# A cached attention block on one core: K loaded by pairs of packs in 16 KB rows, the query weights loaded without a staging copy

## The chip, the cores and the metric

The kernel runs on one core of a Trainium2 chip. The metric is device time in microseconds of one execution. Besides the times there is a profile of one execution: a trace of every instruction, of the DMA packets and of the semaphores.

## What is computed

Two independent blocks A and B, each an attention layer with a cache, their outputs side by side:

```
B, Sq, D = 16, 64, 640;  H, Sk, Dh = 32, 512, 128        # all bf16
q = (x @ wq).reshape(B, Sq, H, Dh).transpose(0, 2, 1, 3)
scores = einsum("bhqd,bhkd->bhqk", q, k_cache) * Dh ** -0.5
p = softmax(scores, axis=-1)
o = einsum("bhqk,bhkd->bhqd", p, v_cache)
out_block = o.transpose(0, 2, 1, 3).reshape(B, Sq, H * Dh) @ wo
out = concatenate([out_A, out_B], axis=-1)
```

K and V are 67 MB each per block, 268 MB in all; every byte of them is used once. wq and wo are 5.2 MB each per block.

## The kernel before

**Tiling.** The work is cut into 128 packs. A pack is 4 heads of 2 batches: 8 pairs of head and batch, 1 MB (1,048,576 bytes) of K and as much of V. Four packs (NJ = 4) make a group, which shares one tile of x (2 batches, 128 rows of queries). Eight groups, 32 packs, make a phase: all 16 batches for 16 of the 32 heads of a block. There are four phases (A, A, B, B), and each has its own half of wq and wo: 2.6 MB of each.

**The steps of a pack n**, by the kinds under which the planner lists them:

- QP (L688, TensorE): q from xT and wq, 20 matmuls; QE (L694, ScalarE) copies it out.
- KT (L702, VectorE): K of the pack, 128 x 2048 words of 4 bytes, is transposed in blocks of 32 x 32 from kn_ring to kt_ring. A word is two neighbouring bf16 of one key.
- S (L712, TensorE): the scores; EX (L741, ScalarE): exp with row sums; RC (VectorE): reciprocals; NM (L762, POOL): normalization.
- TR (L774, TensorE): transposes of the normalized pack; TE (L854, VectorE, two copies): pT from PSUM.
- PV (L867, TensorE): times V; OE (L875) and ZO (L879, ScalarE).
- OP (L887, TensorE): times wo, summed up over the four packs of a group; OS (L897, L900, VectorE) takes the sum once per group.

**Order of work.** Nothing is scheduled at run time. `build_plan` gives each step a time in units of packs (the table AT: KT of pack n at n - 0.672, S at n, TR at n + 1.293, TE at n + 1.432 and n + 1.47, PV at n + 1.701, and so on), sorts each engine's list by it, and works out the semaphore waits from what each step reads and writes. Each engine works through its list in order. TensorE's and ScalarE's lists run as loops of four packs.

**Loads.** All loads but the first x are issued by SP, in order of a list of their own (`loads`). V of pack n stands at n - 2.1 and waits for the ring of four V buffers: for PV of pack n-4, told by the end of the TR of pack n-3. K of pack n stands at n - 4.6; its ring kn_ring has six packs. From pack 8 on, a pack's K is two DMAs of 512 KB in rows of 8 KB, and V is one DMA of 1 MB in rows of 4 KB; packs before 8 have four and two smaller ones. wo is loaded per pack and phase (L621, 640 KB).

**wq** is loaded in five DMAs per phase, in rows of 4 KB, to a staging tile ws_sb (L615). The step WP (L656, POOL, 1.26 us) copies it, twice for each of the four packs of a group, to wqp_sb with its columns in another order; QP reads wqp_sb. The five loads of a later phase are spread over the phase before; those of the first phase are the first loads of all.

**The layout.** In a pack, partition 4 (h p) + 2 b + l of kn_ring holds 32 keys of one head and batch: a row of 8 KB. The columns of wqp_sb are ordered so that q's rows match the order in which the transpose leaves the columns of K.

**Zeroing.** Before the first pack VectorE zeroes two V buffers (VZ, L594), four PSUM banks (BZ, L598), half of wo_sb (WZ, L602) and pT (TE of pack -2, L852), so that steps for the packs -2 and -1, which don't exist, do no harm. POOL zeroes one pn buffer (NM of pack -1, L760).

After the last pack of the main program the kernel looks at a flag and would run a second, more general program if row sums were out of range; here it isn't run.

Of the kernel before, what the change touches and what calls it, by code (L numbers as in the profile page):

```python
# [20 lines left out]
class Cfg:  # L21
    NK = 6
    NV = 4
    NKT = 2
# [9 lines left out]
    NARROW = 2  # L34
    AFTER = 24
# [5 lines left out]
              OPZ=(1.65, 1.7), OSH=(1.75, 1.8), STH=(1.85, 1.9), FL1=1.3, FLM=1.68, FLC=1.82, WP0=(-1.6, -1.59, -0.7, -0.69, 0.25, 0.26, 1.25, 1.26),  # L41
              WP1=(-3.5, -2.55, -2.45, -1.5, -0.5, 0.5, 0.6, 1.5))
# [44 lines left out]
def build_plan(dims, cfg, general):  # L87
# [7 lines left out]
    AT = cfg.AT  # L95
    ops = []
# [9 lines left out]
    def add_output(n):  # L106
# [27 lines left out]
        for b in range(2):  # L134
            add("dve", "TE", (n, b), n + AT["TE"][b], [], [("B", 4 + b), ("pT", b, 0), ("pT", b, 1)])
# [36 lines left out]
    for ph in range(NPH):  # L172
        twp = [ph * PH + t for t in AT["WP1" if ph else "WP0"]]
        for kt in range(dims["KT"]):
            ready = (twp[-1] - PH if ph > 1 else AT["WP0"][-1]) + 0.5
            op = add("sp", "LDWQ", (ph, kt), twp[0] - 0.5 if ph else -20.0, [], [("ws", kt, j) for j in range(NJ)])
            loads.append((ready + 2.0 + 0.14 * PH * kt if ph > 1 else AT["PV"] + 0.15 if ph else -50.0, 1, op))
        for j in range(NJ):
            w = ph * NJ + j
            n0 = ph * PH + j  # L180
            for i in range(2):
                add("pool", "WP", (w, i), twp[2 * j + i], [("ws", kt, j) for kt in range(dims["KT"])], [("wqp", j, i)])
            if ph:
                loads.append((n0 - NJ + AT["LDWO"], 4, add("sp", "LDWO", w, n0 + AT["OP"] - 0.8 * NJ, [], [("wo", j)])))
            else:
                loads.append((n0 - 1.9, 4, add("sp", "LDWO", w, n0 + AT["OP"] - 0.8 * NJ, [], [("wo", j)])))
    if not general:
        add("pool", "PZ", 0, -9.95, [], [("zeros",)])
    add("dve", "VZ", 0, -9.9, [], [("v", i % cfg.NV, b) for i in (-2, -1) for b in range(2)])
    add("dve", "BZ", 0, -9.8, [], [("B", 4), ("B", 5), ("B", 6), ("B", 7)])  # L190
    add("dve", "WZ", 0, -9.7, [], [("wo", NJ - 2), ("wo", NJ - 1)])
    add("pool", "NM", -1, -1 + AT["NM"][3], [], [("pn", -1 % cfg.NPN, i) for i in range(4)])
    for n in range(-2, N):
# [4 lines left out]
        add("pe", "QP", n, n + AT["QP"], [("xT", g % cfg.NX), ("wqp", j, 0), ("wqp", j, 1)], [("SB", 1)])  # L198
        add("act", "QE", n, n + AT["QE"], [], [("SB", 1), ("qs", n % cfg.NQ)])
        for i in range(4):  # L200
            if i < 2 or n < cfg.KSPLIT:
                op = add("sp", "LDK", (n, i), n + AT["KT"] - 0.9, [], [("kn", n % cfg.NK)])
                loads.append((n - cfg.NV + AT["PV"] + 0.2 - cfg.KLEAD, 2, op))
        add("dve", "KT", n, n + AT["KT"], [("kn", n % cfg.NK)], [("kt", n % cfg.NKT)])
        add("pe", "S", n, n + AT["S"], [("qs", n % cfg.NQ), ("kt", n % cfg.NKT)],
# [47 lines left out]
    for op in ops:  # L253
# [9 lines left out]
        if op.kind == "QP" and op.idx > 0:  # L263
            op.deps = [d for d in op.deps if d.kind != "WP"]
# [3 lines left out]
    def for_pe(d):  # L268
        if d.kind == "EX":
            return d.idx % 4 == 1 or d.idx % 4 == 0 and d.idx // 4 % NJ == 1  # L270
        if d.kind == "OE":
            return d.idx[1] == 0
        if d.kind == "LDV":
            return d.idx[1] == 1
        if d.kind == "NM":
            return d.idx % 4 == 3 and d.eng == "pool"
        if d.kind == "OS" and d.idx == N // NJ - 1:
            return False
        return d.kind in own

    def stand_in(d, op):
        if op.eng == "pe":
# [4 lines left out]
            if d.kind == "OE":  # L287
                return d if d.idx[1] == 0 else at[("ZO", d.idx[0])]
            if d.kind in ("EX", "MX") and not for_pe(d):
                if op.kind == "S":  # L290
                    return at[("QE", op.idx)]
                return d if id(op) not in inside and d.kind == "EX" else None
            return d
        if d.kind == "PV" and op.eng == "sp":
            return at[("TR", d.idx + 1)]
        if d.kind == "QP" and op.eng == "pool":
            return at[("TR", d.idx - 1)]
        if d.kind == "XT" and op.eng == "sp":
            return at[("XE", d.idx)]
        if d.kind == "OS" and op.eng == "sp" and for_pe(d):  # L300
            return at[("RC", (d.idx * NJ + NJ + 1, 1))]
        if not for_pe(d):
# [3 lines left out]
        if d.kind == "KT":  # L306
            return at[("S", d.idx)]
# [34 lines left out]
    for op in ops:  # L342
        if op.kind == "LDK":
            packs.setdefault(op.idx[0], []).append(op)
            op.group = packs[op.idx[0]]
# [159 lines left out]
def mha_kernel(nc, blocks, out, cfg=None):  # L505
# [18 lines left out]

    plans = []
# [6 lines left out]
    with contextlib.ExitStack() as es:  # L532
# [5 lines left out]
        wqp_sb = sb("wqp_sb", [128, NJ, KT, 512], BF16)  # L538
        wo_sb = sb("wo_sb", [128, HPH, D], BF16)
        ws_sb = sb("ws_sb", [128, KT, NJ, 512], BF16)  # L540
        kn_ring = sb("kn_ring", [128, NK, 2, 2048], BF16)
        kt_ring = sb("kt_ring", [128, NKT, 32, 2, 2, 16, 2], BF16)
# [68 lines left out]
        def em_LDWQ(e, op):  # L611
# [3 lines left out]
            ins = e.dma_start(ws_sb[:, i].rearrange("p j c -> p (j c)"), src[:, i, c:c + NJ * 512])  # L615
# [8 lines left out]
        def em_LDK(e, op):  # L624
            n, b, l = op.idx[0], op.idx[1] // 2, op.idx[1] % 2
            blk, bp, j, h = pack_info(n)
            src = blocks[blk][1][2 * bp:2 * bp + 2, h:h + 4].rearrange("b h (p l t) d -> l (h p) b (t d)", l=2, t=32)[l]
            if n < cfg.KSPLIT:
                ins = e.dma_start(kn_ring[2 * b + l::4, n % NK].rearrange("p a c -> p (a c)"), src[:, b])
            else:  # L630
                ins = e.dma_start(kn_ring[l::2, n % NK].rearrange("p a c -> p (a c)"), src)  # L631
            return ins, ins

        def em_LDV(e, op):
# [15 lines left out]
            return ins, ins  # L650

        def em_WP(e, op):
            j, jj = op.idx[0] % NJ, op.idx[1]
            src = ws_sb[:, :, j].rearrange("p k (i j r) -> p k i j r", i=4, j=2)
            dst = wqp_sb[:, j].rearrange("p k (i r j two) -> p k i j r two", i=4, j=2, two=2)
            ins = e.tensor_copy(dst[:, :, :, jj], src[:, :, :, jj].rearrange("p k i (r two) -> p k i r two", two=2))  # L656
# [23 lines left out]
        def em_QP(e, op):  # L680
# [4 lines left out]
            w = wqp_sb[:, j].rearrange("p k (c f) -> p k f c", f=4)  # L685
# [12 lines left out]
        def em_KT(e, op):  # L698
            n = op.idx
            dst = kt_ring[:, n % NKT].rearrange("p t j b k two -> p (t j) b (k two)").bitcast(F32)  # L700
            src = kn_ring[:, n % NK].rearrange("p a c -> p (a c)").bitcast(F32).rearrange("p (c h b l) -> p c h b l", h=8, b=2, l=2)
            ins = e.transpose(dst.rearrange("p c b (h l) -> p c h b l", h=8, l=2), src)  # L702
            return ins, ins

        def em_S(e, op):
            n = op.idx
            first = last = None
            for f in range(4):
                for b in range(2):
                    for i in range(4):  # L710
                        rows = slice(32 * i, 32 * i + 32)
                        last = e.matmul(ps[64 * b:64 * b + 64, i, :], qs_ring[rows, n % NQ, f, b, :],  # L712
                                        kt_ring[rows, n % NKT, :, f // 2, b, :, f % 2],
# [16 lines left out]
        def exp_views(h):  # L730
            u = 2 if wide(h // 4) else 4
            return (ps[:, h % 4, :].rearrange("q (u t p) -> q t p u", u=u, p=16),
# [199 lines left out]
        ahead = {}  # L932

# [3 lines left out]
        def emit(e, op, p, taken):  # L937
# [3 lines left out]
            if waits and not op.dma and op.kind != "FL1":  # L941
                attach = waits.pop()
            for s, v in waits:
                e.wait_ge(sem[s], v * units(s))
            kind = "EXG" if p and op.kind == "EX" else op.kind
            first, last = emitters[kind](e, op)
            if last is None:
# [123 lines left out]
```

## Time and profile before

| | |
|---|---|
| median of 3 runs | 732.01 us (731.84 to 732.11) |
| the profiled execution | 732.12 us |
| its span, first to last instruction | 730.4 us |
| mean granted TensorE clock | 0.99 |
| TensorE busy | 674.1 us (92%) |
| VectorE busy | 514.5 us (70%) |
| ScalarE busy | 533.3 us (73%) |
| POOL busy | 417.9 us (57%) |
| moved by DMA | 295.02 MB, mean 404 GB/s |

The span is cut into 40 slices on the page; a digit is the busy share of a slice in tenths. L702 and the like are line numbers of the kernel before. In a row of the order of time stand start, length, engine, line, operation, out<-in, shape and count, and in brackets how long the engine was idle before it and what ended that. The chain of waits follows the work that ended last back to what released it. The profile's DMA share is the mean busy share of the 16 DMA engines that move all data.

### The profile page before, as it was taken

What the parts mean: (1) busy time and instruction counts of PE and PEld (TensorE: products, weight loads), DVE (VectorE), ACT (ScalarE), POOL (GpSimd) and SP (SyncE); (2) the same over time, 40 slices, a digit from 0 to 9 for tenths busy, and PEclk for the clock granted to TensorE, in tenths of its full rate; (3) what the DMA queues carried; (4) which work ended last, traced back from release to release, by engine and by line L of the source; (5) the groups of instructions that cost most, each with busy time, mean ns of one, the idle gap of its engine ahead of it and who ended that gap; (6) DMA issues with size and microseconds to landing.
All of it is one profiled execution on the core that took longest, in us unless ns stands there. A gap on an engine that the chain in (4) does not pass through costs nothing.

```text
span 730.4 us, 61195 instructions
## 1 busy us (share of the span) xinstructions
PE 674.1 (92%) x28502; PEld 530.3 (73%) x28502; DVE 514.5 (70%) x691; ACT 533.3 (73%) x1574; POOL 417.9 (57%) x596
## 2 busy tenths in 40 slices
PE   1679999999999999999997899999999799999998
PEld 1458778787777777777775677787777577787775
DVE  5447777777777766767765667677777567878775
ACT  1447878778787777777875677777778677878775
POOL 4436565666875455554884555465587446555552
PEclk9889999999999999999999999999999999999999
DMA  8999999999999999999999999999999999999993
GB/s 337 401 404 414 414 415 413 415 414 415 415 400 409 419 414 416 416 416 417 416 411 402 415 414 413 414 415 415 414 416 407 403 415 418 417 418 417 416 415 122
DMA packets 72336, 295.02 MB, mean 404 GB/s; under 512 B 7664, under 2 KB 20080, under 8 KB 55920
## 3 DMA queue, kind: packets, MB, share of 16 engines
q1 hardware_dynamic: 72160, 294.52, 100.0%
q8 instruction: 10, 0.16, 0.1%
q10 hardware_dynamic: 144, 0.16, 0.1%
q14 instruction: 22, 0.18, 0.1%
HBM read 292.03 MB, written 2.62 MB: 403 GB/s over the span
## 4 chain that ended last, share of the span: by engine, by line
PE 53%; DMA 32%; SPq 6%; DVE 3%; issue 3%; POOL 2%; ACT 1%; DVEq 0%; POOLq 0%
DMA xn_ring<-in_B_x_dram 14%; PE ps L867 12%; PE ps L887 11%; PE ps L688 11%; PE ps L712 10%; DMA kn_ring<-in_A_k_cache_dram 9%; PE ps L774 7%; DMA kn_ring<-in_B_k_cache_dram 5%; DMA wo_sb<-in_B_wo_dram 4%; SPq L631 4%; DVE kt_ring L702 2%; POOL pn_ring L762 2%; SPq L641 1%; DVE pT_sb L854 1%; SPq L615 1%
## 5 line engine op out<-in xcount | busy, mean ns | idle before, releaser
L762 POOL TENSOR_SCALAR pn_ring<-pn_ring,recip 128x512 bf16<-128x512 bf16 x508 | 343.4, 695 | 246.1 <-DVE recip L754 221.0
L702 DVE STREAM_TRANSPOSE kt_ring<-kn_ring 128x2048 f32<-128x2048 f32 x128 | 295.3, 2307 | 120.3 <-DMA kn_ring<-in_B_k_cache_dram 80.3
L741 ACT ACTIVATE pn_ring<-ps 128x512 bf16<-128x512 f32 x512 | 296.4, 592 | 5.7 <-PE ps L712 5.7
L854 DVE COPY pT_sb<-ps 128x1024 bf16<-128x1024 bf16 x256 | 168.4, 671 | 60.2 <-PE ps L774 60.2
L688 PE MATMUL ps<-xT_ring,wqp_sb 128*128 128x128 bf16 x2560 | 165.9, 220 | 11.6 <-POOL xT_ring L677 11.6
L867 PE MATMUL ps<-pT_sb,v_ring 32*128 32x64 bf16 x16448 | 162.2, 192 | 10.6 <-DVE pT_sb L854 4.6
L688 PEld LDWEIGHTS ps<-xT_ring,wqp_sb 128*128 128x128 bf16 x2560 | 157.5, 114 | 17.8 <-issue 11.8
L867 PEld LDWEIGHTS ps<-pT_sb,v_ring 32*128 32x128 bf16 x16448 | 147.0, 91 | 24.8 <-issue 12.5
L887 PE MATMUL ps<-wo_sb,oT_sb 128*128 128x320 bf16 x1024 | 163.5, 303 | 0.0
L875 ACT ACTIVATE oT_sb<-ps 128x256 bf16<-128x256 f32 x257 | 84.7, 381 | 95.1 <-PE ps L867 95.1
L712 PE MATMUL ps<-kt_ring,qs_ring 32*64 32x512 bf16 x4096 | 138.4, 380 | 4.8 <-issue 4.8
L694 ACT ACTIVATE qs_ring<-ps 128x512 bf16<-128x512 f32 x128 | 76.4, 597 | 76.5 <-PE ps L688 74.5
L774 PEld LDWEIGHTS ps<-ident,pn_ring 64*128 64x128 bf16 x4096 | 68.3, 95 | 77.0 <-ACT oT_sb L875 46.0
L887 PEld LDWEIGHTS ps<-wo_sb,oT_sb 128*128 128x128 bf16 x1024 | 90.4, 98 | 36.7
L741 ACT ACTIVATION_READ_ACCUMULATOR pn_ring<-ps 128x1 f32 x512 | 105.3, 206 | 0.0
L774 PE MATMUL ps<-ident,pn_ring 64*128 64x64 bf16 x4096 | 82.9, 191 | 22.8 <-POOL pn_ring L762 18.6
L712 PEld LDWEIGHTS ps<-kt_ring,qs_ring 32*64 32x64 bf16 x4096 | 53.4, 103 | 32.9 <-issue 5.5
L754 DVE RECIPROCAL recip<-rowsum 128x2 f32<-128x2 f32 x256 | 40.6, 158 | 27.6 <-ACT pn_ring L741 24.6
L879 ACT ACTIVATE ps<-zeros 128x256 f32<-128x256 bf16 x128 | 49.5, 387 | 4.1
L656 POOL COPY wqp_sb<-ws_sb 128x1280 bf16<-128x1280 bf16 x32 | 39.6, 1256 | 9.9 <-DMA ws_sb<-in_A_wq_dram 6.8
L668 ACT ACTIVATE xe_sb<-ps 128x640 bf16<-128x640 bf16 x32 | 22.9, 716 | 8.7 <-PE ps L662 8.6
L677 POOL COPY xT_ring<-xe_sb 128x640 bf16<-128x640 bf16 x16 | 11.5, 717 | 21.0 <-PE ps L774 21.0
(42 smaller groups left out, 103.5 us busy)
## 6 DMA issues: line engine op xcount, KB each, us to landing
kn_ring<-in_B_k_cache_dram SPq DMA_DIRECT2D x128, 512.0 KB, 16.1
v_ring<-in_B_v_cache_dram SPq DMA_DIRECT2D x62, 1024.0 KB, 16.5
kn_ring<-in_A_k_cache_dram SPq DMA_DIRECT2D x112, 512.0 KB, 11.4
v_ring<-in_A_v_cache_dram SPq DMA_DIRECT2D x56, 1024.0 KB, 14.8
kn_ring<-in_A_k_cache_dram SPq DMA_DIRECT2D x32, 256.0 KB, 8.6
v_ring<-in_A_v_cache_dram SPq DMA_DIRECT2D x16, 512.0 KB, 8.9
ws_sb<-in_A_wq_dram SPq DMA_DIRECT2D x10, 512.0 KB, 9.3
wo_sb<-in_A_wo_dram SPq DMA_DIRECT2D x8, 640.0 KB, 13.3
```

The costliest lines, as they stand in the source:

```text
L688: last = e.matmul(ps[:, 1, f * 128:(f + 1) * 128], w[:, kt, f, :], xT_ring[:, xs, kt, :], start=(kt == 0), stop=(kt == KT - 1))
L694: ins = e.activation(qs_ring[:, op.idx % NQ].rearrange("p f b q -> p (f b q)"), ps[:, 1, :], ACTF.Copy, scale=scale)
L702: ins = e.transpose(dst.rearrange("p c b (h l) -> p c h b l", h=8, l=2), src)
L712: last = e.matmul(ps[64 * b:64 * b + 64, i, :], qs_ring[rows, n % NQ, f, b, :], kt_ring[rows, n % NKT, :, f // 2, b, :, f % 2], start=(f = ...
L741: ins = e.activation(dst, src, ACTF.Exp, scale=1.0, accum_out=sum_of(h))
L762: ins = e.tensor_scalar(pn_view(h), pn_view(h), recip[:, h:h + 1], 1.0, ALU.mult, ALU.mult)
L774: last = e.transpose(pt_bank(b)[:, 64 * c:64 * c + 64], pn[rows, c, :], ident[rows, rows], tile_position=(64 * b, 0))
L854: ins = e.tensor_copy(pT_sb[:, b].rearrange("p t q -> p (t q)"), pt_bank(b))
L867: last = e.matmul(ps[:, 4 + i, 64 * b:64 * b + 64], v_ring[rows, n % NV, b, c, :], pT_sb[rows, b, c, :], start=(t == 0 and i < 2), stop=(t ...
L875: ins = e.activation(oT_sb[:, 2 * a:2 * a + 2, :], o_ps[:, 2 * a:2 * a + 2, :], ACTF.Copy)
L879: ins = e.activation(z_ps, zeros[:, :].unsqueeze(2).broadcast_to([128, 2, 128]), ACTF.Copy)
L887: last = e.matmul(out_ps[:, s, :], oT_sb[:, i, :], wo_sb[:, 4 * j + i, s * NH0:(s + 1) * NH0], start=(j == 0 and i == 0), stop=(j == NJ - ...
```

## The change

Four things are changed together.

1. **K by pairs.** Packs 2 to 119 (FROM = 2, the last ALONE = 8 left out) are loaded and transposed by pairs (n, n+1), n even. A pack's K is still two DMAs of 512 KB, but in rows of 16 KB: 64 keys of one head and batch on one partition, so that a pack fills 64 of the 128 partitions (every other pair of partitions) and two packs share one slot. kn_ring has 3 slots of two packs (as many bytes as before), kt_ring 2 of two packs (twice the bytes). A pair takes two transposes of 128 x 2048 words; each takes one half of the words of a key (every second word) from both packs. The first stands at n - 1.672 in VectorE's list and the second at n - 0.672; both packs' K must have landed for the first. Packs 0, 1 and 120 to 127 take four K DMAs of 256 KB in rows of 8 KB and two transposes of half the size each.
2. **K's place in SP's list.** Of a pair, both loads stand at n - 5.6; before, at n - 4.6 and n - 3.6. The first pairs have times of their own.
3. **wq unstaged.** ws_sb and WP go. wq is loaded straight to wqp_sb, in two DMAs per phase of 1.3 MB in rows of 2 KB; the order of columns that WP made is now in the transpose of K. In the first phase K of pack 0 stands between the two. In a later phase that begins at pack n they stand at n - 4.4 and n - 2.4 in SP's list, and since they overwrite what QP reads, SP waits for the QP of the second and of the fourth pack of the group before (a mark that TensorE's next step raises). The waits for their landing are put on a new step GO ahead of the first QP, on XC (xT's copy, POOL) and on the last NM of a group's first pack (POOL).
4. **Zeroing.** WZ goes from VectorE to POOL, behind the first XC; pT is zeroed just before the first KT.

The views of ScalarE's exp change with the order of the keys (4 runs of 8 rather than 2 of 16 in the inner loop), the shapes don't.

```diff
-    NK = 6
+    NK = 3
+    FROM = 2
+    ALONE = 8
...
-            add("dve", "TE", (n, b), n + AT["TE"][b], [], [("B", 4 + b), ("pT", b, 0), ("pT", b, 1)])
+            add("dve", "TE", (n, b), n + AT["TE"][b] if n > -2 else AT["KT"] - 0.01 + 0.002 * b, [], ...)
...
-        for kt in range(dims["KT"]):
...
+        for i in range(2):
+            op = add("sp", "LDWQ", (ph, i), ph * PH + 2 * i + AT["WQ"][0] if ph else -20.0, [],
+                     [("wqp", j) for j in (2 * i, 2 * i + 1)])
+            loads.append((ph * PH + 2 * i + AT["WQ"][1] if ph else (-50.0, -4.0)[i], 1, op))
...
-                add("pool", "WP", (w, i), twp[2 * j + i], [("ws", kt, j) for kt in range(dims["KT"])], [("wqp", j, i)])
...
+    add("pe", "GO", 0, AT["QP"] - 0.001)
...
-    add("dve", "WZ", 0, -9.7, [], [("wo", NJ - 2), ("wo", NJ - 1)])
+    add("pool", "WZ", 0, AT["XC"] + 0.001, [], [("wo", NJ - 2), ("wo", NJ - 1)])
...
+        paired, slot = FROM <= n < TO, n // 2 % cfg.NK
+        halves = [("kn", slot, a) for a in ((0, 1) if paired else (n % 2,))]
+        at_k = n - cfg.NV + AT["PV"] + 0.2 - cfg.KLEAD
+        if FROM <= n < FROM + 2 * cfg.NK:
+            at_k = n - n % 2 - 4.75 + n % 2 * 0.05
+        elif FROM <= n < TO + 2 * cfg.NK:
+            at_k -= 1 + n % 2 * 0.95
...
-        add("dve", "KT", n, n + AT["KT"], [("kn", n % cfg.NK)], [("kt", n % cfg.NKT)])
...
+        for j in range(2):
+            tk = n + AT["KT"] + (0.02 * j if not paired else j - 1)
+            if n == TO and not j:
+                tk -= 1
+            if not paired or n % 2 == 0:
+                add("dve", "KT", (n, j), tk, halves, [("kt", n // 2 % cfg.NKT, a, j) for a in ((0, 1) if paired else (n % 2,))])
...
+        if op.kind == "QP":
+            n, j = op.idx, op.idx % NJ
+            at[("GO", 0) if n < 2 else ("XC", n // NJ) if j < 2 else ("NM", 4 * (n - j) + 3)].deps += [d for d in op.deps if d.kind == "LDWQ"]
+            op.deps = [d for d in op.deps if d.kind != "LDWQ"]
...
+            if paired(n):
+                ins = e.dma_start(slot[2 * (n % 2) + o::4].rearrange("p a c -> p (a c)"),
+                                  src.rearrange("b h (p o t) d -> o (h p) b (t d)", o=2, t=64)[o])
...
+            src = kn_ring[:, n // 2 % NK].bitcast(F32)
+            if paired(n):
+                src = src.rearrange("p a (t k b e o j) -> p j (a t) k b e o", k=4, b=2, e=2, o=2, j=2)[:, j]
+                dst = dst.rearrange("p e b t (k o) -> p t k b e o", o=2)
```

More of the change, by code (lines that the diff above doesn't have):

```diff
@@ L932, in mha_kernel @@
         ahead = {}
+        marks = []
         def units(key):
@@ L940, in emit @@
             attach = None
-            if waits and not op.dma and op.kind != "FL1":
+            if waits and not op.dma and op.kind not in ("FL1", "GO"):
                 attach = waits.pop()
```

93 lines of the change are left out of this document (51 added, 42 removed).

## The prediction, made before the result was known

> **What bounds the kernel now.** I read the page first, then the busy time by windows (here four of them), then the chain that ended last (pieces as start, length, what), then the waits (total us, times, longest), and last the order of time around the latest DMA that the chain names.
>
> ```profile
> span 730.4 us, 61195 instructions
> ## 1 busy us (share of the span) xinstructions
> PE 674.1 (92%) x28502; PEld 530.3 (73%) x28502; DVE 514.5 (70%) x691; ACT 533.3 (73%) x1574; POOL 417.9 (57%) x596
> ...
> DMA  8999999999999999999999999999999999999993
> ...
> q8 instruction: 10, 0.16, 0.1%
> ```
>
> ```profile
> 0.00:10.00 10.00, 0.69 (x5) 0.45 (x5) 7.33 (x3) 1.99 (x2) 1.45 (x8) 1.00 0.75 268
> 10.00:20.00 10.00, 3.92 (x148) 3.71 (x148) 5.15 (x5) 0.60 (x1) 7.78 (x7) 1.00 1.02 419
> 553.00:585.00 32.00, 26.55 (x1132) 20.97 (x1134) 20.30 (x27) 22.34 (x68) 17.93 (x25) 1.00 1.03 404
> 600.00:632.00 32.00, 31.77 (x1362) 24.77 (x1346) 24.68 (x33) 25.78 (x77) 17.48 (x26) 1.00 1.02 417
> ```
>
> The DMA engines have work in every slice but the last. The last two figures of a window are DMA share and GB/s: from 10 us on the share is above 1.0 (packets overlap a little), so no engine waits for an issue, and bytes come at the rate of the stream. TensorE is 92% busy: two clocks run side by side, the stream's and PE's. The chain and the waits tell which one leads where.
>
> ```profile
> 586.28 18.53 DMA kn_ring<-in_B_k_cache_dram
> 604.83 2.31 DVE kt_ring L702
> 609.25 1.21 PE ps L867 x128
> 612.03 1.19 PE ps L887 x8
> ...
> 714.84 1.19 PE ps L887 x8
> ```
>
> ```profile
> DVE kt_ring L702 <- DMA kn_ring<-in_B_k_cache_dram: 80.3, 64, 2.8
> ```
>
> The last DMA in the chain is a K load that lands at 604.83. Behind it stands PE alone: from the output projection at 612.03 to that at 714.84 there are 20 rounds (21 projections, of which the chain shows first and last), 102.81 / 20 = 5.14 us a pack. So the end is the landing of K at 604.83 plus PE's own pace. Ahead of it the stream leads: the K transpose waited 64 times for K of block B alone, 80.3 us in all.
>
> ```profile
> 599.85 2.31 DVE L702 STREAM_TRANSPOSE kt_ring<-kn_ring 128x2048 f32<-128x2048 f32 x1 [1.43 <-DMA kn_ring<-in_B_k_cache_dram]
> ...
> 604.83 2.31 DVE L702 STREAM_TRANSPOSE kt_ring<-kn_ring 128x2048 f32<-128x2048 f32 x1 [1.30 <-DMA kn_ring<-in_B_k_cache_dram]
> ```
>
> ```profile
> 604.79 1.07 PE L712 MATMUL ps<-kt_ring,qs_ring 32*64 32x512 bf16 x32
> ...
> 610.39 1.07 PE L712 MATMUL ps<-kt_ring,qs_ring 32*64 32x512 bf16 x32
> ```
>
> ```profile
> L702 DVE STREAM_TRANSPOSE kt_ring<-kn_ring x22: 2312/2314/2315, 604.8 to 712.7; 128x2048 f32<-128x2048 f32 x22
> ```
>
> From 604.83 on there are 22 transposes, and the last is that of pack 127: the one at 604.83 belongs to pack 106, the one at 599.85 to pack 105. Their score matmuls (L712) start at 604.79 (105) and 610.39 (106). A transpose that waits holds up the copies of pT behind it on VectorE, and those hold up PV (L867), which stands just ahead of the scores.
>
> **The cost of pairing: one slot earlier.** In the list of VectorE, the transpose of pack n stands now at n - 0.672. For a pair (n, n+1), n even, the first of two transposes stands at n - 1.672, which is the slot that pack n-1 has now, and it needs K of both packs. K is moved ahead in SP's list to make up for it: K(n) now follows V(n-3) in the stream, and would follow V(n-4), with K(n+1) right behind. The bytes that must have landed are then the same: now K to n and V to n-3, (n+1) + (n-2) loads of 1 MB; after, K to n+1 and V to n-4, (n+2) + (n-3). The same place in the stream thus opens a slot that comes one pack earlier in the work. For pack 106: the bytes that land at 604.83 let the transpose of the slot before run. In that slot it is 604.79 - 599.85 = 4.94 us from the transpose to the scores of 105, then a round of 5.14 to those of 106, 10.08 in all; now it is 610.39 - 604.83 = 5.56. PE is later by 10.08 - 5.56 = 4.5 us against the stream. It is not below nothing, since VectorE works in order; it is not above the full round of 5.14. Behind 604.83 PE runs at its own pace, so what it is late there it is late at the end; the last 8 packs, which stay unpaired, give nothing back, since PE can't run faster than 5.14.
>
> **The gain: fewer packets.** What a packet costs beyond its bytes comes from two windows. The four wo loads of the last phase fall in 553 to 585:
>
> ```profile
> L621 SPq DMA_DIRECT2D wo_sb<-in_B_wo_dram x4: 589/592/725, 545.0 to 568.9; - x4
> ...
> DMA to landing us min/median/max: 14.6/14.8/18.1
> ```
>
> They are 4 x 655 KB in rows of 1280 B (640 columns of 2 bytes), 2048 packets; a pack of K and V is 2.097 MB in 128 rows of 8 KB and 256 of 4 KB. So 553:585 moved 32 x 404 = 12.93 MB in 2048 + 10.31 / 2.097 x 384 = 3935 packets, and 600:632 moved 13.34 MB in 2443. Both took 16 x 32 us of engine time: 1492 packets more against 416 KB less. With a per packet and b per KB, 1492 a = 416 b and 2443 a + 13,344 b = 512,000 ns: b = 36.5 and a = 10 ns (9 to 11 by the rounding of GB/s). K in 16 KB rows is 64 packets a pack, not 128. Up to pack 107, 106 packs are paired: 106 x 64 x 10 / 16 = 4.2 us less. wq goes from rows of 4 KB to rows of 2 KB, 640 more packets in each of 4 phases, all ahead of pack 106: 2560 x 10 / 16 = 1.6 us more. Net 2.6 us less. No 16 KB data row stands in the trace. Bounds: nothing saved, if such a row moves as two of 8 KB; above, the ten instruction packets of 16 KB (q8), 0.1% of 16 x 730 us, or 1.2 us each where 36.5 x 16.4 + 10 = 0.61 is expected. [...]
>
> [...]
>
> **The rest.**
>
> ```profile
> L656 POOL COPY wqp_sb<-ws_sb 128x1280 bf16<-128x1280 bf16 x32 | 39.6, 1256 | 9.9 <-DMA ws_sb<-in_A_wq_dram 6.8
> ...
> kn_ring<-in_B_k_cache_dram SPq DMA_DIRECT2D x128, 512.0 KB, 16.1
> ```
>
> ```profile
> 3.37 8.96 SPq L629 DMA_DIRECT2D kn_ring<-in_A_k_cache_dram  x12
> ...
> 7.90 2.19 DVE L602 MEMSET wo_sb<- 128x2560 uint32 x1 [0.52 <-issue]
> ...
> 14.83 2.31 DVE L702 STREAM_TRANSPOSE kt_ring<-kn_ring 128x2048 f32<-128x2048 f32 x1 [4.74 <-DMA kn_ring<-in_A_k_cache_dram]
> ```
>
> ```profile
> L760 POOL MEMSET pn_ring<- x1: 1805/1805/1805, 17.7 to 17.7; 128x2048 bf16 x1
> ```
>
> Head: with half of wq (1.31 MB) behind K(0), the first transpose comes 1.31 / 0.417 = 3.1 us sooner (at 417 GB/s), and the 39.6 us of wq copies leave POOL. I count both at nothing: the stream runs from some 2.5 us in either way and carries the same bytes to pack 106. If PE's start got worse and the stream ran dry, each idle microsecond would cost one. In the head, by the order of time and the rows of L656 and L760 above: zeroing wo on POOL is 5120 elements where pn has 2048: 4.5 us for 2.2 on DVE, behind xT and ahead of pn's zeros, which now wait until 17.7: covered. K(0), K(1) are two transposes of half size each; between half of 2.31 and a whole one, 0 to 2.3 us a pack; in the last 8 packs VectorE has (the 1.43 and 1.30 us of idle time in front of its transposes) about 1.3 us of room. I take nothing, and 0.5 in the range. Their four issues a pack (8.96 / 12 = 0.75 us each) fit in 5.14.
>
> At a phase's start wq overwrites what QP still reads: SP waits for the QP of the second (fourth) pack of the last group, up to 1.3 packs or 6.6 us, and V, the K pair and wo are queued behind. K loads take 16.1 us to land, so that much is in flight: cover enough, no cost; without it some 6 us at each of 3 phases. Who waits for wq: xT's copy and a pack's last normalization on POOL. Its first half stands behind K(n+1), V(n-3) for a phase that begins at pack n, and xT's copy is at n - 0.788; the pair behind it needs more of the stream at about the same time. So K stays what is late.
>
> **Sum.** +4.5 - 2.6 = +1.9 us on the span of 730.4. The profiled execution took 732.12 (1.7 around the span), the median of three runs is 732.01. So 734.0. This case's own range: a from 6 to 14 ns, 1.6 to 3.7 us saved; the slot 4.0 to 5.1: 732.4 to 736.
>
> **Rivals.** *The slot costs nothing* (faster). If the end hangs on the last landing and not on PE, the 118 paired packs save 118 x 64 x 10 / 16 = 4.7, less 1.6 for wq: 729.0. For it: the last V is issued at 710.0 and took 10.4 to land, 10 us before the end, with little room:
>
> ```profile
> L648 SPq DMA_DIRECT2D v_ring<-in_B_v_cache_dram x4: 368/422/472, 704.5 to 710.0; - x4
> ...
> DMA to landing us min/median/max: 10.4/12.0/12.9
> ```
>
> Against it: the chain holds no DMA after 604.83. It decides if K of a pair lands some 4.5 us before its slot. 0.24, in which I count the case that 16 KB rows save well over 10 ns.
> *16 KB rows save nothing*, being moved as two of 8 KB: +4.5 + 1.6 = +6.1, 738.2. Rows of 8 KB are the largest that the kernel loads now, so nothing here excludes it. 0.11.
> *The transpose slows down*: it reads every second 4-byte word where it reads whole rows now. DVE has 514.5 / 128 = 4.0 us a pack; from 2312 + 1100 ns on it is the slowest engine, and at twice 2312 a pack takes 6.3, 118 x 1.2 = 140 us more. [...] 0.04. With it goes the case that 16 KB rows cost 1.2 us like the instruction packets: 7552 rows x 0.6 / 16, 280 us more. 0.02.
>
> My forecast has 0.59. About 0.2%, 1.5 us, is what a measurement of this kernel can tell from no change. The forecast's range begins at +0.4, so 0.17 of it is no change and 0.42 slower. Faster 0.24; same 0.17; slower 0.42 + 0.17 = 0.59. The range for 8 in 10 takes in both near rivals: 728.6 to 738.6.
>
> **What would show it.** Fewer packets of 8 KB or less by some 12,500 (15,104 K rows become 7552 of 16 KB, wq adds 2560), GB/s up by 2 to 3 in the stretches without wo. The transposes that wait for K are the first of each pair, every second one, and the last DMA in the chain is K of a pair near pack 106, with scores some 10 us behind it where it is 5.6 now. L702 keeps 2.31 us, L656 is gone, and the first transpose starts near 11.7. I am wrong if K pairs land before their slots at the end, if DMA share falls below 1.0 between 10 and 700 us, or if 16 KB rows give the same GB/s as now.

## The result and the profile after

The changed kernel takes 1155.76 us (median, 1142.76 to 1173.03), the kernel before 731.93 in the same series: the ratio is 1.567, 95% interval 1.560 to 1.574. The ratio goes by the two faster of the four runs (1142.76 and 1151.47 us); the other two, one of them the profiled one, are over 1.5% above the fastest and count as slow. The forecast was 734.0, its range 728.6 to 738.6. The profiled execution of the kernel after took 1160.05 us, its span is 1158.3.

From the page of the kernel after:

```profile
span 1158.3 us, 61159 instructions
...
PE 787.3 (68%) x28502; PEld 590.7 (51%) x28502; DVE 507.2 (44%) x700; ACT 541.0 (47%) x1574; POOL 383.9 (33%) x565
...
DMA  9999999999989999999899999999999999999994
...
DMA packets 67216, 295.02 MB, mean 255 GB/s; under 512 B 7536, under 2 KB 19952, under 8 KB 58352
...
DMA 75%; PE 15%; SPq 7%; issue 2%; DVE 1%; ACT 0%; POOL 0%; DVEq 0%
```

Of the same kernel, four views: the busy time by windows (length; each engine's busy time; clock, DMA share, GB/s), the chain near its end, the group of the large transposes, and the DMA issues of block B's K by pairs (count, KB each, median us from issue to landing). Line numbers are now those of the kernel after: L730 is K's transpose, L740 the scores' matmul, L895 PV.

```profile
10.00:20.00 10.00, 6.18 (x203) 4.09 (x201) 2.37 (x2) 3.45 (x11) 2.16 (x2) 1.00 1.06 306
600.00:632.00 32.00, 17.38 (x605) 12.39 (x606) 12.93 (x17) 10.81 (x31) 8.87 (x13) 0.73 1.03 265
200.00:700.00 500.00, 334.87 (x11950) 250.63 (x11950) 210.56 (x285) 227.32 (x662) 159.48 (x235) 0.81 1.00 254
```

```profile
1080.96 27.41 DMA v_ring<-in_B_v_cache_dram
1108.42 1.73 PE ps L895 x128
...
1120.75 20.47 DMA kn_ring<-in_B_k_cache_dram
1141.24 2.37 DVE kt_ring L730 x2
```

```profile
L730 DVE STREAM_TRANSPOSE kt_ring<-kn_ring 128x2048 f32<-128x2048 f32 x118 | 271.6, 2302 | 376.0 <-DMA kn_ring<-in_A_k_cache_dram 192.2 <-DMA kn_ring<-in_B_k_cache_dram 183.8
```

```profile
kn_ring<-in_B_k_cache_dram SPq DMA_DIRECT2D x112, 512.0 KB, 20.2
```

The digits of the DMA engines look as before, and the DMA share is 1.00 to 1.06, as before. The last figure of a window differs: 265 GB/s in 600 to 632 us where it was 417. The DMA engines are not idle, they are slow: the packets of the loads took 99.0% of 16 engines' span, 100.0% before. The same 295.02 MB go at 255 GB/s on the mean, 404 before, and the stream sets the time: TensorE (PE) has become the one that waits (68% busy), and the chain, PE alone at the end before, is DMA to the last K. On its way there it stands mostly in loads of V, 63% of the span.

The granted clock of TensorE fell as well (0.81 from 200 to 700 us, 1.00 before), and its busy time rose from 674.1 to 787.3 us. That is still far below the span, and K's loads alone, with no matmul beside them, are slow in the same way (266 GB/s, e1_probe). The transposes keep 2.30 us but wait 376 us for K, whose loads of 512 KB take 20.2 us to land in block B, 16.1 before.

By the packets' own records in the trace, a K packet of 16 KB took 1.06 us on the mean, where the prediction expected 0.61. Packets that the change did not touch became slower too: V's of 4 KB took 0.246 us, 0.163 before.

### The profile page after: what moved, and what is told of

It reads as the page before. It is cut to its first block, busy times and chain, and to the rows that moved or that the text cites. A ratio compares the mean times of both kernels' runs of the same rounds, so it can differ in the third digit from the quotient of the medians.

```text
span 1158.3 us, 61159 instructions
## 1 busy us (share of the span) xinstructions
PE 787.3 (68%) x28502; PEld 590.7 (51%) x28502; DVE 507.2 (44%) x700; ACT 541.0 (47%) x1574; POOL 383.9 (33%) x565
## 2 busy tenths in 40 slices
DMA packets 67216, 295.02 MB, mean 255 GB/s; under 512 B 7536, under 2 KB 19952, under 8 KB 58352
## 4 chain that ended last, share of the span: by engine, by line
DMA 75%; PE 15%; SPq 7%; issue 2%; DVE 1%; ACT 0%; POOL 0%; DVEq 0%
DMA v_ring<-in_A_v_cache_dram 33%; DMA v_ring<-in_B_v_cache_dram 30%; PE ps L895 5%; PE ps L740 4%; DMA wo_sb<-in_B_wo_dram 4%; PE ps L802 2%; SPq L656 2%; DMA wqp_sb<-in_B_wq_dram 2%; DMA wo_sb<-in_A_wo_dram 2%; DMA kn_ring<-in_A_k_cache_dram 2%; DMA kn_ring<-in_B_k_cache_dram 2%; SPq L670 2%; PE ps L915 1%; PE ps L710 1%; SPq L934 1%
## 5 line engine op out<-in xcount | busy, mean ns | idle before, releaser
L730 DVE STREAM_TRANSPOSE kt_ring<-kn_ring 128x2048 f32<-128x2048 f32 (+1 forms) x138 | 295.2, 2145 | 384.2 <-DMA kn_ring<-in_A_k_cache_dram 195.5
L895 PE MATMUL ps<-pT_sb,v_ring 32*128 32x64 bf16 x16448 | 193.3, 210 | 288.8 <-DMA v_ring<-in_B_v_cache_dram 129.7
L895 PEld LDWEIGHTS ps<-pT_sb,v_ring 32*128 32x128 bf16 x16448 | 176.6, 105 | 305.2 <-DMA v_ring<-in_A_v_cache_dram 140.8
L740 PE MATMUL ps<-kt_ring,qs_ring 32*64 32x512 bf16 x4096 | 184.0, 482 | 6.5 <-issue 6.5
L915 PE MATMUL ps<-wo_sb,oT_sb 128*128 128x320 bf16 x1024 | 179.3, 323 | 0.0
L802 PEld LDWEIGHTS ps<-ident,pn_ring 64*128 64x128 bf16 x4096 | 79.6, 103 | 135.7 <-issue 91.3
L802 PE MATMUL ps<-ident,pn_ring 64*128 64x64 bf16 x4096 | 95.5, 203 | 62.4 <-POOL pn_ring L790 55.0
L915 PEld LDWEIGHTS ps<-wo_sb,oT_sb 128*128 128x128 bf16 x1024 | 96.0, 104 | 45.7
L740 PEld LDWEIGHTS ps<-kt_ring,qs_ring 32*64 32x64 bf16 x4096 | 61.8, 123 | 54.9 <-issue 32.7
L699 POOL COPY xT_ring<-xs_sb 128x640 bf16<-128x640 bf16 x16 | 11.5, 717 | 53.7 <-PE ps L802 45.0
## 6 DMA issues: line engine op xcount, KB each, us to landing
kn_ring<-in_B_k_cache_dram SPq DMA_DIRECT2D x112, 512.0 KB, 20.2
```

Of the source, the lines that this page charges most:

```text
L730: ins = e.transpose(dst, src)
L802: last = e.transpose(pt_bank(b)[:, 64 * c:64 * c + 64], pn[rows, c, :], ident[rows, rows], tile_position=(64 * b, 0))
L895: last = e.matmul(ps[:, 4 + i, 64 * b:64 * b + 64], v_ring[rows, n % NV, b, c, :], pT_sb[rows, b, c, :], start=(t == 0 and i < 2), stop=(t ...
L915: last = e.matmul(out_ps[:, s, :], oT_sb[:, i, :], wo_sb[:, 4 * j + i, s * NH0:(s + 1) * NH0], start=(j == 0 and i == 0), stop=(j == NJ - ...
```

## The experiments

Three theories stood at first: rows of 16 KB are slow by their length; the source of 16 x 2 rows (16 rows of each of two batches in one DMA) is slow; reading every second row is slow.

**e1_probe: the loads alone, one shape after another.** 8.4 MB in each stage.

```
wide8   as before: 64 rows of 8 KB, source 32 x 2          new8   as after, unpaired: 32 rows of 8 KB, source 16 x 2
old8    as before, first packs: 32 rows of 8 KB, one dim   new16  as after, pairs: 32 rows of 16 KB, source 16 x 2
swap16  32 rows of 16 KB, one dim     skip16  32 rows of 16 KB, every second row of 8 heads, one dim
all16   128 rows of 16 KB             all4    128 x 2 rows of 4 KB (as V)          wide8 again
```

> This kernel computes no attention: it writes zeros and only loads K, 8 MB (8.4 million bytes) per stage, one stage after the other, in nine shapes; it tells the time of a packet in each. Rows of 8 KB: as before from pack 8 on (64 partitions, source 32 x 2 rows), as before in the first packs (32 partitions, source 32 rows in one dimension), as the changed kernel loads unpaired packs (32 partitions, source 16 x 2 rows). Rows of 16 KB: as the changed kernel loads pairs (source 16 x 2), the same partitions from 32 rows in one dimension that follow each other, the same from 32 rows of which every second one is read, and all 128 partitions. Then V's rows of 4 KB, and the first shape again. Theory 1, the length: a packet of 16 KB is slow in itself (1.06 us in the changed kernel against 0.31 for 8 KB before). Then all four shapes of 16 KB take about 1.0 us a packet and some 250 GB/s, and all three of 8 KB about 0.31 and 417. Theory 2, the split: slow is what has 16 x 2 rows, whatever their length, since the unpaired packs of the changed kernel, 8 KB, took 0.47 us with no 16 KB packet near. Then the two shapes with 16 x 2 rows are slow, 0.47 us and 1.06 us a packet (around 250 to 280 GB/s), and the other two of 32 partitions and the one of 128 take 0.31 and 0.62, at 415 to 425 GB/s. Theory 3, the addresses: reading every second row of 16 KB is slow; then the shape that skips rows is slow as well and the one whose rows follow each other is not.

Windows inside the stages, in the order of the list above (wide8, old8, new8, new16, swap16, skip16, all16, all4, wide8); columns are length, POOL, clock, DMA share, GB/s:

```profile
3.00:22.00 19.00, 0.00 (x0) 1.00 1.00 404
27.00:47.00 20.00, 0.00 (x0) 1.00 0.97 378
52.00:78.00 26.00, 0.00 (x0) 1.00 1.00 282
84.00:113.00 29.00, 0.00 (x0) 1.00 1.00 266
118.00:136.00 18.00, 0.00 (x0) 1.00 0.99 413
141.00:160.00 19.00, 0.00 (x0) 1.00 0.99 412
165.00:182.00 17.00, 0.00 (x0) 1.00 1.01 431
187.00:205.00 18.00, 0.00 (x0) 1.00 1.02 412
210.00:228.00 18.00, 0.00 (x0) 1.00 1.00 404
```

Rows of 16 KB reach 413 to 431 GB/s, reading every second row 412. Only the two stages with 16 x 2 rows are slow, the one with 8 KB too. The median packet of 16 KB took 611 ns in swap16, skip16 and all16, and 984 in new16. Length and addresses fall.

**e3_half: the kernel after, each K row of 16 KB loaded as two of 8 KB, still 16 x 2.**

```diff
-                ins = e.dma_start(slot[...], src.rearrange("b h (p o t) d -> o (h p) b (t d)", o=2, t=64)[o])
+                # once for each half of t (32 keys, 8 KB)
```

> The changed kernel with each row of 16 KB loaded as two of 8 KB by DMAs of their own (four of 256 KB per paired pack, source 16 x 2 rows as before this edit). Theory 1 (length): the packets take 0.31 us again and the time is 735 to 742. Theory 2 (split): the packets take about 0.47 us and K stays slow; around 1050 to 1150. Theory 3 (addresses): between, some 1100.

One run, 1045.75 us. Half the length does not bring the rate back. By the packets' own records one of K with 8 KB took 0.484 us, so that 16 KB took 0.97 where they took 1.06, and one of V 0.214 where it took 0.246. Over 16 engines that is 43 us less for K and 65 for V, about the 110 us by which this run is shorter than the kernel after. Why both are less slow is not explained.

**e2_swap: the kernel after with two bits of the partition changed over.** A K load now fills every fourth partition from 32 rows of one batch.

```diff
-                                  src.rearrange("b h (p o t) d -> o (h p) b (t d)", o=2, t=64)[o])
+                                  src[o].rearrange("h (p t) d -> (h p) (t d)", t=64))
...
-                dst = dst.rearrange("p e b t (k o) -> p t k b e o", o=2)
+                dst = dst.rearrange("p e b t (k o) -> p t k o e b", o=2)
```

> The changed kernel with two bits of K's partition changed over: the batch and the half of a run of 128 keys. A pair's pack is still two DMAs of 512 KB in rows of 16 KB to 32 partitions each, but a DMA reads one batch, 32 rows in one dimension, where it read 16 x 2. Theory 1 (length): nothing changes, about 1150 us, 16 KB packets at 1.06 us. Theory 2 (split): the stream runs at 417 GB/s or more again, 16 KB packets at 0.62 us, and the time is what the prediction's sum gave for the change without this fault, 734 (732.4 to 736). Theory 3 (addresses of every second row): also about 734, since the rows of one DMA follow each other here.

753.71 us, ratio to before 1.030 (1.028 to 1.032): 402 us of the 424 are gone. By the records of the packets, K's 16 KB took 616 ns and V's 4 KB 165 again. The difference in packet time between the two kernels, over 16 engines: K 7552 x (1061 - 616) = 210 us, V's 4 KB 32,256 x (246 - 165) = 163, the shorter ones and the 8 KB rows 42: 415 us, beside 407 between the two spans (1158.3 and 751.2). V thus pays nearly as much as K for K's loads. From the page of e2_swap, with the groups of the transposes and of the scores' matmul:

```profile
PE 691.0 (92%) x28502; PEld 537.8 (72%) x28502; DVE 682.3 (91%) x700; ACT 536.5 (71%) x1574; POOL 382.2 (51%) x565
...
DMA packets 67216, 295.02 MB, mean 393 GB/s; under 512 B 7536, under 2 KB 19952, under 8 KB 58352
...
PE 60%; DMA 15%; DVE 13%; SPq 5%; ACT 2%; issue 2%; POOL 0%; ACTq 0%; DVEq 0%
```

```profile
L730 DVE STREAM_TRANSPOSE kt_ring<-kn_ring 128x2048 f32<-128x2048 f32 x118 | 453.0, 3839 | 32.0 <-DMA kn_ring<-in_B_k_cache_dram 17.4 <-DMA kn_ring<-in_A_k_cache_dram 14.6
L740 PE MATMUL ps<-kt_ring,qs_ring 32*64 32x512 bf16 x4096 | 144.9, 394 | 3.4 <-issue 3.4
```

The lowest bit of the partition is now the batch, so neighbouring words of the transpose's output go to places 2 KB apart, where pairs of words went side by side: 3.84 us for 2.30, and VectorE is 682 us busy (91%), where it was 507. It has become a limit beside TensorE; the chain of this run names TensorE for 60% of the span and VectorE for 13%, so how much of the 21 us that are left is VectorE's is not separated from the other terms of the change.

**e4_words, e10_line, e11_two: three layouts of K^T that should make the swap cheap.** b is the batch, o and k the key within a row block; the last bracket is what lies side by side in kt_ring, in words of 4 bytes.

```diff
-  e2_swap   b t (k o)          # b far apart
+  e4_words  t (k o b)          # b side by side
+  e10_line  t (k b o)          # 16 bytes hold both b, two words of each
+  e11_two   t c (b k o)        # 16 bytes of one b, then 16 of the other
```

> The changed kernel with the two partition bits swapped, so that each K load of a pair is 32 rows of 16 KB in one dimension, and with kt_ring laid out so that VectorE writes pairs of 4-byte words again (the scores' matmul then reads its K with a step of 8 bytes, not 4). Theory (the source shape was the whole loss, and the single-word writes were the rest): packets of 16 KB at 611 ns, transposes of 128x2048 back at 2.30 us, and the prediction's sum holds with the probe's packet price: the slot +4.5, packets 7552 x 7 to 9 ns / 16 = -3.3 to -4.2, wq +1.1 to 1.6: 733.5 to 735 us beside 732. Rival 'the slot costs nothing': 729 to 730.5. Rival 'the matmul pays for a read step of 8 bytes': matmuls of the scores longer than 1.07 us per group and a time over 740.

> The kernel of run e4_words with K^T laid out so that VectorE writes the four words of a 16-byte group one after another (in the order 0, 2, 1, 3) and the scores' matmul reads two neighbouring words of every four. If the matmul pays by how many of its columns lie in 16 bytes, its L740 stays near 620 ns and the time near 820 us. If it pays by its innermost step (4 bytes again), L740 is back near 380 to 394 ns; the transposes are then 2.30 us if nearness within 16 bytes suffices for VectorE, 3.84 us if it needs ascending pairs. With both good, the prediction's sum is tested: 733.5 to 735, or 729 to 730.5 if the slot costs nothing.

> As e10_line, but VectorE's words alternate between two neighbouring 16-byte groups, and the matmul reads whole groups of 16 bytes, every second one. If the matmul pays by columns in 16 bytes, L740 is back near 380 to 394 ns here and not in e10_line. Transposes 2.30 us if VectorE joins words over 32 bytes, 3.84 us if not; with 3.84 us VectorE is the bound again, as in e2_swap, near 754 us.

823.73, 824.02 and 754.28 us (ratios 1.125 (1.123 to 1.126), 1.126 (1.124 to 1.127), 1.030 (1.028 to 1.031)). The groups of the scores' matmul (L740) and of the transposes (L730), for e4_words, e10_line and e11_two in turn:

```profile
L740 PE MATMUL ps<-kt_ring,qs_ring 32*64 32x512 bf16 x4096 | 255.6, 622 | 3.7 <-issue 3.7
L730 DVE STREAM_TRANSPOSE kt_ring<-kn_ring 128x2048 f32<-128x2048 f32 x118 | 270.8, 2295 | 13.6 <-DMA kn_ring<-in_A_k_cache_dram 11.0 <-DMA kn_ring<-in_B_k_cache_dram 2.4
```

```profile
L730 DVE STREAM_TRANSPOSE kt_ring<-kn_ring 128x2048 f32<-128x2048 f32 x118 | 270.7, 2294 | 12.6 <-DMA kn_ring<-in_A_k_cache_dram 10.5 <-DMA kn_ring<-in_B_k_cache_dram 2.1
L740 PE MATMUL ps<-kt_ring,qs_ring 32*64 32x512 bf16 x4096 | 255.4, 622 | 3.7 <-issue 3.7
```

```profile
L730 DVE STREAM_TRANSPOSE kt_ring<-kn_ring 128x2048 f32<-128x2048 f32 x118 | 459.8, 3897 | 30.0 <-DMA kn_ring<-in_B_k_cache_dram 15.2 <-DMA kn_ring<-in_A_k_cache_dram 14.8
L740 PE MATMUL ps<-kt_ring,qs_ring 32*64 32x512 bf16 x4096 | 145.9, 395 | 3.4 <-issue 3.4
```

Of each pair of rows, one is good and one bad. VectorE took 2.30 us where two words that it writes in a row fall into the same 16 bytes, side by side (e4) or 8 bytes apart (e10), 3.90 where they alternate between two neighbouring groups of 16 bytes (e11), and 3.84 at 2 KB apart (e2). The matmul took 394 to 395 ns where all four words of 16 bytes are its own (e2, e11), and 622 where only two are, whether apart (e4) or side by side (e10). None of the four swapped layouts has both: with the batch as the lowest bit of the partition, VectorE's neighbours are the two batches, and a matmul reads one. So the swap mends the stream and brings a loss on VectorE or on PE; with the other terms of the change the kernel ends 21 to 22 or 91 to 92 us above the one before.

**e5_late and e6_alone**, built on e4_words and its slow matmuls.

```diff
  e5_late:   FROM = 0, ALONE = 0;  tk = n + AT["KT"] + 0.17 * j      # both transposes of a pair in pack n's slot
  e6_alone:  ALONE = 126                                             # no pairs but the last two packs
```

> The kernel of run e4_words with both transposes of a pair in the slot of its first pack, one right behind the other, and all packs in pairs, the first ones too. If the slot that comes one pack earlier costs 4.5 us, as the prediction has it, this is 4 to 5 us faster than e4_words: 729 to 730.5. If the slot costs nothing, it is within 1 us of e4_words. If two transposes in a row (4.6 us) hold up the copies behind them on VectorE, it is slower than e4_words, by up to 64 x 2.3 = 147 us.

> The kernel of run e4_words with no pairs but the last two packs: K of every pack comes alone in four loads of 256 KB, 32 rows of 8 KB in one dimension, and two transposes of half size each; wq unstaged and the zeroing as in the changed kernel. It is the second and third part of the change alone, but for the four small loads. By the prediction's terms: wq +1.1 to 1.6 us, two half transposes 0 to +0.5: 733 to 734.5 us. If the first half of wq at a phase's start holds K up (6 us at each of 3 phases), 738 to 750. If the copies of wq gone from POOL are worth something, below 731.

911.09 us (ratio 1.244, 1.242 to 1.246) and 828.00 (1.131, 1.129 to 1.132). With PE 96% busy in e4_words (822.0 us of span) neither can say anything on the terms of the prediction's sum. That e5_late is 87 us slower than e4_words, with transposes that waited only 5.3 us for K, speaks for two transposes in a row holding up the work behind them; it was not taken apart further.

**e7_ports and e12_turns: what about 16 x 2 is slow?** Loads alone, rows of 16 KB, all but new16 from sources in one dimension.

```
step4  32 rows on partitions 0, 4, .. 124     new16  as in e1_probe               few8   16 rows on partitions 0, 8, .. 120
step2  32 rows on partitions 0, 2, .. 62      step1  32 rows on 32 neighbours     low64  64 rows on partitions 0 to 63
all64  64 rows on partitions 0, 2, .. 126     alt8   few8, and the same 4 partitions further, in turn
swing  step1 on the first, third, second, fourth quarter in turn
```

> No attention: it loads K rows of 16 KB in stages of one shape each and writes zeros. Stages: step4 (32 rows in one dimension on every fourth partition), new16 (16 x 2 rows, as in the changed kernel), few8 (16 rows in one dimension on every eighth partition), step2 (32 rows on every second partition of the first 64), step1 (32 rows on 32 neighbouring partitions), low64 (64 rows on the first 64 partitions), all64 (64 rows on every second partition), step4 again. Theory P (what costs is which partitions are written at one time: several DMA engines write the same part of SBUF): few8, step2, step1 and low64 are as slow as new16, 0.95 us or more for a packet, and step4 and all64 take 0.61. Theory S (what costs is a source of 16 x 2 rows as such, whatever partitions it goes to): only new16 is slow, and all the others take 0.61.

> No attention: it loads K rows of 16 KB in stages of one shape each and writes zeros. [...] Theory P1 (the engines go through the DMAs in step, so what one DMA's rows share at one time decides): alt8 like new16, 240 GB/s or less, swing about 210 GB/s. Theory P2 (the engines drift apart and later DMAs fill in the idle parts): alt8 and swing near 400 GB/s. If the source of 16 x 2 rows itself matters beside the partitions, alt8 is well over new16.

The windows of e7_ports, in the order step4, new16, few8, step2, step1, low64, all64, step4, and then those of e12_turns, in the order step4, few8, alt8, new16, swing:

```profile
2.00:22.00 20.00, 0.00 (x0) 1.00 0.99 404
26.00:59.00 33.00, 0.00 (x0) 1.00 1.01 245
63.00:82.00 19.00, 0.00 (x0) 1.00 1.02 213
85.00:105.00 20.00, 0.00 (x0) 1.00 1.01 210
108.00:127.00 19.00, 0.00 (x0) 1.00 1.01 210
130.00:150.00 20.00, 0.00 (x0) 1.00 1.01 210
153.00:172.00 19.00, 0.00 (x0) 1.00 0.99 418
176.00:195.00 19.00, 0.00 (x0) 1.00 0.99 414
```

```profile
2.00:22.00 20.00, 0.00 (x0) 1.00 0.98 401
27.00:45.00 18.00, 0.00 (x0) 1.00 1.02 207
48.00:63.00 15.00, 0.00 (x0) 1.00 1.02 258
70.00:100.00 30.00, 0.00 (x0) 1.00 1.01 234
107.00:145.00 38.00, 0.00 (x0) 1.00 0.98 213
```

64 rows on every second partition run at 418 GB/s, 64 such rows on the first 64 partitions at 210. 32 or 64 rows on the lower half, or 16 on every eighth partition: 207 to 213, half the rate, from a plain source. alt8 sends plain sources to the places that new16 writes, one DMA for each half, and is about as slow (258 beside 234 and 245). So a plain source is as slow when its rows go to these places in this order, and in e1_probe sources of 32 x 2 and 128 x 2 rows were fast (404 and 412): the places are enough to explain new16. No stage had 16 x 2 rows in other places. By these rates, which partitions are written at one time counts, and DMAs queued behind, with partitions that would fill the gap, did not bring the rate back (alt8 258, swing 213): theory P, nearest to its form P1.

new16 and step4 fill the same partitions with one DMA, every fourth of the 128, and run at 234 to 266 GB/s and at 401 to 414. In new16 the 16 rows of one batch go to every eighth partition (0, 8, .. 120) and those of the other batch 4 further. What would fit is that the rows of one batch are written at one time, so that it goes as in few8 (207 to 213) and alt8 (258). That order was argued from alt8, not seen: no view tells which engine wrote which partition. It leaves a question open, too: in the same order of places the 32 rows of step4 would be as slow, and they are not. So rows in one dimension would have to be shared out otherwise, and no run here shows whether or how.

**e8_rest and e9_slot: the other terms of the sum, with K loaded as before.** e8_rest is the kernel before with wq unstaged and the zeroing of the change; e9_slot adds the slot that comes one pack earlier.

```diff
  e8_rest:  wq and zeroing as in the change; K's two halves transposed apart (2 x 128x1024), loads of K as before
+ e9_slot:  KT = -1.672 (-0.672), KLEAD = 3.5 (2.5), NKT = 4 (2)
```

> The kernel before with the other two parts of the change alone: wq straight into its place in rows of 2 KB, its first half ahead of K, no copies on GpSimd, and zeroing in the order of need. K comes in the loads and slots of before; each transpose is two of half size, since without the copies wq is not permuted. By the prediction's terms: 2560 more packets at 7 to 10 ns / 16 = +1.1 to +1.6, two half transposes for one 0 to +0.5 (twice 1.22 us for 2.31): 733 to 734. Rival, SP's wait for the last QP of a group holds K up at 3 phases: 738 to 750. Rival, the copies gone from GpSimd or the earlier first transpose bring PE's start forward: 729 to 731.

> The kernel of run e8_rest with every transpose of K one slot earlier in VectorE's list (n - 1.672 for n - 0.672), K one place earlier in the stream for it, and four K^T buffers for two, so that no transpose waits for scores. The packets are those of e8_rest. If the slot that comes one pack earlier costs 4.5 us, as the prediction has it, this is 4 to 5.1 us slower than e8_rest. If the slot costs nothing, it is within 1 us of it. If the room gained lets PE start its work sooner, it is faster.

735.59 us (ratio 1.0049, 1.0035 to 1.0063) and 738.43 (1.0090, 1.0075 to 1.0106). wq and zeroing, with the two half transposes, cost 3.8 us, the slot 2.8 more; by the ends of the two intervals the slot is between 0.9 and 5.2. Both differences are small, but clear of the noise. In the orders of time of the two runs the slot shows as forecast: from the start of the last transpose that the chain names to its own pack's scores e9_slot takes 10.3 us (621.40 to 631.70) and e8_rest 5.6 (630.65 to 636.27).

For e8_rest, SP's order of time at the start of the second phase, and two windows, the first of which lies behind a wait of SP:

```profile
172.88 1.18 SPq L634 DMA_DIRECT2D kn_ring<-in_A_k_cache_dram  x2
179.93 0.37 SPq L618 DMA_DIRECT2D wqp_sb<-in_A_wq_dram  x1
180.35 0.54 SPq L644 DMA_DIRECT2D v_ring<-in_A_v_cache_dram  x1
```

```profile
180.00:185.00 5.00, 5.00 (x209) 3.96 (x193) 4.25 (x8) 4.35 (x13) 2.06 (x4) 1.00 0.88 308
185.00:190.00 5.00, 5.00 (x222) 3.97 (x220) 3.78 (x7) 4.02 (x13) 2.96 (x5) 1.00 1.02 419
```

SP issues nothing from 174.06 to 179.93, while it waits for the QP that still reads wq. What is in flight runs out, and the DMA share falls to 0.88: 5 x (415 - 308) / 415 = 1.3 us of stream are lost. Before, wq had a place of its own and was spread over the phase ahead. At the two later phases the share stays at 1.0 or above in windows of the same length. The packets of 2 KB are the other part: by the packets' records those of 2 KB take 29.0 us more of the 16 engines' time than before, and those of 4 KB 25.6 less, 3.4 us in all. Together 4.7, as much as this profiled span is longer than the one before (735.1 and 730.4); by the medians it is 3.8. This is an account, not a test: the zeroing, the copies gone from POOL and the half transposes changed in the same run.

## Why the prediction was wrong, step by step

**The gain: fewer packets.** This is the step that failed. The prediction called a pack's K "64 packets a pack, not 128", priced a packet by its bytes plus 10 ns, and got 4.2 us less. The price itself held in three stages of e1_probe, at 412 to 431 GB/s: 16 KB took 611 ns in the median in swap16, skip16 and all16, as expected, and twice the 309 ns of an 8 KB row is 7 ns more, beside the 10 taken. But a price per length can't tell where the rows go. The change also turned 64 partitions per DMA, on every second one, into 32 filled in the order of 16 x 2, and that was never looked at, neither here nor among the bounds. A packet of K costs 1.06 us for 0.61, and V is slowed as well: instead of 4.2 us less for fewer packets, some 415 us more of packet time stand in the kernel after than in e2_swap, whose K packets are as long and as many.

**The bounds of that step.** That the line through rows of 8 KB and less, 0.61 us, holds at 16 KB was an estimate. The upper bound, 1.2 us from the instruction packets (1.07 on the mean by their own records in the trace of before), gave a rival of 280 us more with a chance of 0.02. It comes nearest to the result, but its reason, the length, is refuted by e1_probe and e3_half. The rival that 16 KB rows save nothing is refuted by e1_probe's 611 ns, 7 less than two of 8 KB.

**The rest: wq and zeroing.** A term that was sized too small: 1.6 us were taken and 3.8 measured. The prediction saw the wait ("SP waits for the QP", up to 6.6 us; here 5.9) and took K in flight for "cover enough, no cost". In the second phase it was not, at a loss of 1.3 us. The 10 ns a packet were too little for 2 KB rows: by the packets' records 3.4 us where 1.6 stood.

**The slot.** 4.5 us taken, 2.8 measured (0.9 to 5.2), with K loaded as before. The distance on which it rests is seen (10.3 and 5.6 us to the scores, where 10.08 and 5.56 stood), and the rival in which the slot costs nothing falls there; the size is told no closer. In the pairs themselves it was not measured: each of those kernels has a larger loss of its own.

**The transposes.** Right: 2302 ns, though they read every second word; the rival in which they slow down fell for the reads. For the writes it came true in e2_swap, where the mended stream is paid for on VectorE (3.84 us).

**The signs named beforehand.** 12,672 packets of 8 KB or less went (72,336 to 59,664, with 7552 of 16 KB added), the first transpose started at 11.8 (11.7 forecast), the copies of wq are gone, and every second transpose waits for K (56 of 118). Two signs failed: GB/s fell instead of rising by 2 to 3, and the last DMA in the chain is K of one of the last packs, at 1141.24, not of a pair near pack 106. A third gave no warning: a DMA share below 1.0 was to show that the prediction is wrong, and it stayed at 1.0 while the rate fell by 37%.

No version here beats the kernel before: with the stream whole, the pairs end at 753.71 at best, and the two other parts of the change lose 3.8 us by themselves (e8_rest).

## What to carry to other kernels

Cost a DMA by where its rows land and in which order, not only by how long they are: 32 rows of 16 KB went at 210 GB/s to 32 neighbouring partitions and at 401 to 414 to every fourth (e7_ports, e12_turns). If a DMA's destination or the order of its rows changes, measure that shape alone before anything is built on it. A DMA share of 1.0 says that the engines have work, not that they are fast (1.00 at 266 GB/s in new16 and at 404 in wide8, e1_probe), so read GB/s beside it. A layout of the partitions fixes the DMA's writes, VectorE's writes and the matmul's reads all at once; in each of the four swapped layouts here, the bit that was moved for the DMA was paid for by one of the other two (transposes of 3.84 and 3.90 us for 2.30, or score matmuls of 622 ns for 394), so check all three.

## What the runs showed of the hardware that was not expected

- Rows of 16 KB to 32 or 64 partitions of the lower half, or to 16 on every eighth, went at 207 to 213 GB/s, and to every second or fourth of all 128 at 401 to 418 (e7_ports, e12_turns); as 16 x 2 rows on every fourth partition they went at 234 to 266 (also e1_probe), and that the order of the rows is the reason was argued above, not shown. Other loads in flight were slower with it: V's packets of 4 KB took 246 ns in the kernel after, 165 in e2_swap.
- A transpose of 128 x 2048 words took 2.30 us where two words written in a row go to the same 16 bytes (after, e4_words, e10_line), and 3.84 to 3.90 where they don't (e2_swap, e11_two). Reading every second word, with a step of 8 bytes, cost it nothing (2302 ns in the kernel after, 2307 before).
- The scores' matmul (512 columns) took 394 to 395 ns where it reads every second bf16 of whole groups of 16 bytes (e2_swap, e11_two), and 622 where only half of a group is its own (e4_words, e10_line).
